# The table of tokens by expert: added up on chip by zero-one matmuls in place of scatters to DRAM

## The chip, the cores and the metric

The kernel runs on one core of a Trainium2 chip. The metric is the device time of one execution in microseconds (us). The kernel before was run three times: 811.25, 808.84 and 810.61 us, median 810.61. A further execution was profiled. PE is the matrix engine (TensorE), PEld its weight loads, DVE the vector engine, ACT the scalar engine, POOL GpSimd, SP the engine that issues most DMAs.

## What is computed

Two stages, all in float32. First a block-causal attention with 8 batches, 8 heads, 576 tokens and a head dimension of 64; its output, laid out as 4608 tokens of 512 values, goes into a mixture of experts with one expert a token.

```python
# attention: q, k, v [8, 8, 576, 64], block 64
scores = q @ k.T / 8, masked to block_i >= block_j
attn_out = softmax(scores) @ v
x = attn_out.transpose(0, 2, 1, 3).reshape(4608, 512)
# mixture of experts: E = 8, F = 1024
logits = normed(x) @ normed(expert_emb).T / tau
e = argmax(logits);  gate = softmax(logits)[e]
out[token] = gate * (relu(x[token] @ w1[e]) @ w2[e])
```

## The kernel before, in words

**Attention (0 to about 355 us).** The work is 32 passes, one for each pair of heads of a batch (n = 0 to 31, four a batch). A pass has five parts, each a Python generator: `p` prepares q and k (transposes, L326 to L345), `m` finds row maxima (L361 matmuls, L367 on DVE), `s` makes scores and their exp (five groups of matmuls L422, exp on ACT L429/L431, sums pS on POOL L400/L403), `v` multiplies with v (L457) and sums (L476), `f` finishes (L502 to L538). `l` issues the loads (L225) and stores of finished rows (L576, L578). A plan, a string of these letters written by hand for the first passes, the steady ones (n = 5 to 26) and the last (n = 27 to 31), says which generator takes its next step; `run` (L866) steps them, and the main loop (L879) goes through the passes. So the order of every engine's instructions is fixed by the plan, and parts of different passes lie beside each other. PSUM is used as four double banks (`psm`), taken from the front of a list and given back at its end (L199 to L209); a score group holds one until its exp is done.

**The route.** When the fourth pair of a batch b has finished, `route(b)` (L587) is queued in the list `slow`; the plan's letter `r` takes one of its steps, so it spreads over the passes that follow. It finds each token's expert as a zero-one row `ohb`, ranks the tokens of each expert by small matmuls (L616 to L620), adds a base of its expert (L725, `above`), squares the rows (ACT, L582), and works out in `table_rows` (L740; L745 on POOL, L747 to L752 on DVE) the place of each token in a table of tokens by expert. Tokens lie on 128 partitions, NJ = 5 to a partition for a batch. The table is `table` in DRAM with E x RE x 128 places (E = 8 experts, RE = 36 rows of 128 places for each). L670 to L680 write the batch's token numbers there: five indirect DMAs issued by POOL (L672), one for each of the five columns, one step of the route each. This is done for b = 0 to 6; the last batch is placed otherwise.

**Who reads the table.** `zeros` (L282) clears it at the start by a DMA from POOL (L284). `early_rows` (L708, after batch 5) loads the first rows of expert 0 to `et` (SP, L711), gathers those tokens' values (POOL, L717) and turns them into store indices (L694 to L697). Before the experts' part, L1243 loads the whole table as `tbt` (SP), and L1331 to L1334 transpose it on PE (`tps`) and copy it (`tsb`).

**Mixture of experts (about 358 us to the end).** 34 slots of 128 tokens; for each PE transposes the gathered tokens (L1093), multiplies with both weight matrices (L1122), ACT and DVE work on the result (L1149, L1175, L1181, L1183), POOL gathers (L1085) and stores (L1189) by indirect DMA. Nothing of it changes but the source of L1333.

Of the kernel before, what the change touches and what calls it, by code (L numbers as in the profile page):

```python
# [48 lines left out]
def kernel(  # L49
# [12 lines left out]
    nc = tc.nc  # L62
    B, H, S, D = q.shape
    E, DM, DF = w1.shape
    NT = B * S
    P = 128
    NP = H // 2
    NJ = (S - 64) // P + 1
# [5 lines left out]
    EARLY = 2  # L74
# [6 lines left out]
    dram = ctx.enter_context(tc.tile_pool(name="dram", bufs=1, space=bass.MemoryType.DRAM))  # L81
# [3 lines left out]
    RE = (NT + P - 1) // P  # L85
    NCH = (E * RE + P - 1) // P
    RC = E * RE // NCH
    assert RC * NCH == E * RE
    table = dram.tile([E * RE * P, 1], F32, name="table")


    ident = const.tile([P, P], F32, name="ident")
# [18 lines left out]
    def iota(name, shape, pattern, base=0, cm=0, dt=F32):  # L111
        t = const.tile(shape, dt, name=name)
        nc.gpsimd.iota(t, pattern=pattern, base=base, channel_multiplier=cm, allow_small_or_imprecise_dtypes=True)
        return t
# [3 lines left out]
    tokf = iota("tokf", [P, B, NJ], [[S, B], [P, NJ]], 1, 1)  # L118
    gi = iota("gi", [P, NSLOT], [[1, NSLOT]])
    pio = iota("pio", [P, P], [[1, P]])  # L120
# [12 lines left out]
    drop = const.tile([P, NJ], F32, name="drop")  # L133
# [59 lines left out]
    op = pool(left, "op", 1)  # L193
# [7 lines left out]
    def take_bank():  # L201
        return banks.pop(0) if wide else ps_b.tile([P, 2, 512], F32, name="psb")
# [4 lines left out]
    def give_bank(t):  # L207
        if wide:
            banks.append(t)  # L209
# [55 lines left out]
    nmr = [rt.tile([P, P], F32, name=f"nmr{i}") for i in range(2)]  # L265
    oe = [rt.tile([P, SP], F32, name=f"oe{i}") for i in range(2)]
    su = [rt.tile([P, 2 * P], F32, name=f"su{i}") for i in range(2)]
    zcol = op.tile([P, S], F32, name="zcol")
    nc.vector.memset(zcol, 0.0)

# [10 lines left out]

    def zeros():  # L282
        nc.gpsimd.dma_start(xbuf[0:1, :], zcol[0:1, 0:RW])
        nc.gpsimd.dma_start(table.rearrange("(c p t) o -> p c (t o)", p=RC, t=P),  # L284
                            zcol[0:RC, 0:NCH * P].rearrange("p (c t) -> p c t", t=P))
        for i in range(2):
            nc.gpsimd.memset(oe[i][:, S:SP], 0.0)
            nc.gpsimd.memset(su[i][:, LW:2 * P], 0.0)
        nc.gpsimd.memset(enT, 0.0)
        for i in range(2):  # L290
            nc.gpsimd.memset(ends_v[i][64:P], 0.0)
# [281 lines left out]
    def store_piece():  # L573
        b, xrow, j = pieces.pop(0)
        r0 = b * S + 1 + j * P
        nc.sync.dma_start(xbuf[r0:r0 + P, :], xrow[:, j, :])  # L576
        if j == NJ - 2:
            nc.sync.dma_start(xbuf[r0 + P:r0 + P + 64, :], xrow[0:64, NJ - 1, :])  # L578
# [8 lines left out]
    def route(b, xrow, lgh, ssp):  # L587
# [4 lines left out]
        ohb, acc = hot[b % 2][:, 0:NJ, :], hot[b % 2][:, NJ, :]  # L592
# [17 lines left out]
        rb = take_bank() if wide else ps_m.tile([P, 1, 512], F32, name="psm")  # L610
# [10 lines left out]
        if b < B - 1:  # L621
            t2 = above(rk, ebase)
# [28 lines left out]
        eng.tensor_scalar(ss, ss, 1.0e-6, None, op0=ALU.add)  # L651
        yield
        if b < B - 1:
            rowj = yield from table_rows(t2, ohb)
        nc.vector.reciprocal(ss, ss)
        yield
        eng.tensor_tensor(lg, lg, bc(ss.unsqueeze(2), P, NJ, E), op=ALU.mult)
# [10 lines left out]
            store(b, xrow, (NP - 1) * P, RW)  # L668
        yield
        if b < B - 1:  # L670
            for j in range(NJ):
                w = nc.gpsimd.indirect_dma_start(  # L672
                    out=table, out_offset=bass.IndirectOffsetOnAxis(ap=rowj[:, j:j + 1], axis=0),
                    in_=tokf[:, b, j:j + 1], in_offset=None, bounds_check=E * RE * P - 1, oob_is_err=False)
                for o in writes:
                    tc.declare_no_dep(w.ins, o.ins, reason="each place is written once")
                writes.append(w)
                if (b == B - 2 or j == NJ - 1) and pieces:
                    store_piece()
                yield  # L680
            if b == EB:
                early_g.append(early_rows())

    EB = B - 3
    early_g = []
    writes, ends = [], []
    ei = st.tile([P, 2, EARLY], I32, name="ei")
    ex = [st.tile([P, RW], F32, name=f"ex{u}") for u in range(EARLY)]

# [16 lines left out]
        yield  # L706

    def early_rows():  # L708
        et = rt.tile([P, EARLY], F32, name="et")
        none = rt.tile([P, EARLY], F32, name="enone")  # L710
        nc.sync.dma_start(et, table.rearrange("(p r) o -> p (r o)", p=P)[:, 0:EARLY])  # L711
        yield
        while pieces:
            store_piece()
        nc.gpsimd.tensor_copy(ei[:, 0], et)
        for u in range(EARLY):
            nc.gpsimd.indirect_dma_start(  # L717
                out=ex[u], out_offset=None, in_=xbuf[0:1 + (EB + 1) * S, :],
                in_offset=bass.IndirectOffsetOnAxis(ap=ei[:, 0, u:u + 1], axis=0))
            yield  # L720
        indices(nc.gpsimd, None, ei[:, 1], et, none)

    def above(rk, base):
        t = sm.tile([P, NJ, E], F32, name="t2")
        nc.vector.tensor_tensor(t, rk, base, op=ALU.add)  # L725
        return t
# [12 lines left out]

    def table_rows(t, ohb):  # L740

        row = sm.tile([P, NJ], F32, name="row")
        rowt = sm.tile([P, NJ], I32, name="rowt")
        rowj = sm.tile([P, NJ], I32, name="rowj")
        nc.gpsimd.tensor_tensor(t, t, ohb, op=ALU.mult)  # L745
        yield
        nc.vector.tensor_reduce(rowj, t, axis=AX.X, op=ALU.max)  # L747
        yield
        nc.vector.tensor_scalar(rowt, rowj, P - 1, None, op0=ALU.bitwise_and)
        nc.vector.scalar_tensor_tensor(row, rowj, 1.0 / P, drop, op0=ALU.mult, op1=ALU.add)  # L750
        yield
        nc.vector.scalar_tensor_tensor(rowj, rowt, float(E * RE) - 1.0 / P, row, op0=ALU.mult, op1=ALU.add)  # L752
        yield
        return rowj

    def drain(g, n=None, skip=("pe", "squares", "fine")):
        while g is not None and (n is None or n > 0):
# [82 lines left out]
    for i in range(1, NBUF):  # L840
        init_a(nc.gpsimd, qa[i])
        init_x(nc.gpsimd, qa[i], 1)
    zeros()
    drain(pb, 2)
    fill(1)
# [52 lines left out]
    def flat(ap):  # L898
        return ap.rearrange("p o n -> p (o n)")
# [300 lines left out]
    def chain():  # L1200
# [4 lines left out]
        for c in fg:  # L1205
            if c == "squares":
                break
            yield c
        ch_sq.append(fg)
        rg = route(B - 1, xrow, lgh, ssp)  # L1210
        for c in rg:
            if c == "counted":
# [26 lines left out]
        drain(g)  # L1239
    del slow[:]  # L1240
    ring(0)
    tbt = st.tile([P, NCH * RC], F32, name="tbt")
    nc.sync.dma_start(tbt, table.rearrange("(p r) o -> p (r o)", p=P))  # L1243

    mx = ctx.enter_context(tc.tile_pool(name="mx", bufs=1, reuse_waits="tile"))
    for nm in ("xh", "xl"):
# [78 lines left out]
    a, b = ea  # L1325
# [4 lines left out]
    go()  # L1330
    tps = ps_m.tile([P, 512], F32, name="psm")  # L1331
    for c in range(NCH):
        nc.tensor.transpose(tps[0:RC, c * P:(c + 1) * P], tbt[:, c * RC:(c + 1) * RC], ident)  # L1333
    nc.vector.tensor_copy(tsb, tps[0:RC, 0:NCH * P].rearrange("r (c t) -> r c t", t=P))  # L1334
    def second(c):
        split_lo(1, c, 1, to=0)
# [190 lines left out]
```

## Time and profile before

| | us |
|---|---|
| median of three runs | 810.61 |
| the profiled execution, its own time | 810.42 |
| its span in the profile | 808.7 |
| PE at work | 779.2 (96%) |
| DVE at work | 604.2 (75%) |
| POOL at work | 435.7 (54%) |
| ACT at work | 408.4 (50%) |

The granted clock of TensorE is 1.00 over the span. "Busy" leaves out register, branch and semaphore instructions. A line such as L422 is a line of the kernel. Matmul ends are modelled, so lengths of matmuls overlap; the distance of two starts is the better measure of PE's pace. In a line of the order of instructions, a group "x2" is two like instructions, and what stands in brackets is how long the engine was idle before it and what released it.

### The profile page before, as it was taken

What the parts mean: (1) busy time and instruction counts of PE and PEld (TensorE: products, weight loads), DVE (VectorE), ACT (ScalarE), POOL (GpSimd) and SP (SyncE); (2) the same over time, 40 slices, a digit from 0 to 9 for tenths busy, and PEclk for the clock granted to TensorE, in tenths of its full rate; (3) what the DMA queues carried; (4) which work ended last, traced back from release to release, by engine and by line L of the source; (5) the groups of instructions that cost most, each with busy time, mean ns of one, the idle gap of its engine ahead of it and who ended that gap; (6) DMA issues with size and microseconds to landing.
All of it is one profiled execution on the core that took longest, in us unless ns stands there. A gap on an engine that the chain in (4) does not pass through costs nothing. (4 is left out here: it accounts for less than half of the span.)

```text
span 808.7 us, 23043 instructions
## 1 busy us (share of the span) xinstructions
PE 779.2 (96%) x7160; PEld 627.3 (78%) x7160; DVE 604.2 (75%) x1382; ACT 408.4 (50%) x831; POOL 435.7 (54%) x420
## 2 busy tenths in 40 slices
PE   8999999999999998899999999999999999999997
PEld 3678878787878776668878887788888888888885
DVE  6667878686868776658868777877887778877881
ACT  2566757575757564664744456553533332543222
POOL 7555676767676757772347288784761111661110
PEclk9999999999999999999999999999999999999999
DMA  4745364545454543163845357454441111111111
GB/s 104 169 95 136 84 158 105 147 104 132 101 140 100 141 100 101 29 231 127 297 151 166 100 158 235 152 167 150 148 153 45 55 54 45 38 49 55 54 35 39
DMA packets 141421, 93.95 MB, mean 116 GB/s; under 512 B 118925, under 2 KB 120541, under 8 KB 141260
## 3 DMA queue, kind: packets, MB, share of 16 engines
q1 hardware_dynamic: 133228, 69.74, 31.2%
q0 software_dynamic: 8032, 22.36, 8.7%
q8 instruction: 66, 1.08, 0.6%
q14 instruction: 95, 0.78, 0.3%
HBM read 72.71 MB, written 19.71 MB: 114 GB/s over the span
## 5 line engine op out<-in xcount | busy, mean ns | idle before, releaser
L1175 DVE STREAM_TRANSPOSE pt<-h 32x256 f32<-32x256 f32 x528 | 240.6, 456 | 31.3 <-ACT h L1149 14.1
L367 DVE TENSOR_REDUCE nmx<-psm 128x16 f32<-128x1024 f32 (+2 forms) x128 | 125.6, 986 | 21.4 <-PE psm L361 18.5
L912 POOL TENSOR_TENSOR ring_l<-raw,ring_h 128x1024 f32 (+1 forms) x49 | 116.3, 2406 | 35.7 <-ACT ring_h L907 20.0
L1189 POOL DMA_INDIRECT out_dram<-y,outi x36 | 36.7, 1020 | 176.5 <-ACTq L1061 118.8
L1122 PE MATMUL py<-ring_h,hh 128*128 x272 | 109.3, 402 | 0.7 <-ACT h L1149 0.7
L1122 PE MATMUL py<-ring_l,hh 128*128 x272 | 106.3, 391 | 0.0
L429 ACT ACTIVATE pT<-psm 128x640 f32<-128x640 f32 (+2 forms) x128 | 89.1, 703 | 28.2 <-PE psm L361 16.8
L403 POOL TENSOR_TENSOR pS<-pS,pT 128x640 f32<-128x640 f32 (+2 forms) x93 | 93.5, 1006 | 10.9 <-ACT pT L431 3.2
L1122 PE MATMUL py<-ring_h,hl 128*128 x272 | 88.8, 389 | 0.0
L1122 PE MATMUL ph<-ring_l,xh 128*128 x280 | 86.3, 390 | 0.8 <-POOLq L1073 0.8
L1122 PE MATMUL ph<-ring_h,xh 128*128 x280 | 86.3, 389 | 0.6 <-ACTq L1061 0.6
L457 PE MATMUL psm<-pT,vo 128*64 128x320 f32 (+2 forms) x640 | 76.1, 380 | 1.0 <-issue 1.0
L1188 ACT ACTIVATE y<-py,xg 128x512 f32<-128x512 f32 x34 | 23.4, 689 | 103.5 <-PE py L1122 97.9
L1183 DVE TENSOR_TENSOR hl<-pt,hh 128x512 fp32r<-128x512 f32 x66 | 42.5, 686 | 42.0 <-ACT hh L1181 42.0
L422 PE MATMUL psm<-qh,kh 64*128 64x320 f32 (+4 forms) x384 | 66.5, 341 | 5.9 <-ACT pT L429 3.5
L907 ACT CAST ring_h<-raw 128x1024 f32 (+1 forms) x62 | 61.0, 1050 | 22.1 <-POOLq L1073 11.6
L1181 ACT CAST hh<-pt 128x512 fp32r<-128x512 f32 x66 | 35.5, 590 | 72.1 <-DVE pt L1175 71.7
L1122 PE MATMUL ph<-ring_h,xl 128*128 x280 | 69.2, 389 | 0.0
L457 PEld LDWEIGHTS psm<-pT,vo 128*64 128x64 f32 x640 | 43.2, 137 | 29.3 <-issue 1.9
L1122 PEld LDWEIGHTS ph<-ring_l,xh 128*128 128x128 f32 x280 | 52.5, 188 | 12.1 <-POOLq L1073 1.2
L1122 PEld LDWEIGHTS ph<-ring_h,xh 128*128 128x128 f32 x280 | 52.5, 188 | 11.7 <-ACTq L1061 0.8
L1122 PEld LDWEIGHTS ph<-ring_h,xl 128*128 128x128 f32 x280 | 52.6, 188 | 10.9
(289 smaller groups left out, 1680.7 us busy)
## 6 DMA issues: line engine op xcount, KB each, us to landing
raw<-in_moe_w_dram SPq DMA_DIRECT2D x60, 512.0 KB
qn<-in_q_dram SPq DMA_DIRECT2D x64, 128.0 KB
kn<-in_k_dram SPq DMA_DIRECT2D x64, 128.0 KB
vo<-in_v_dram SPq DMA_DIRECT2D x64, 128.0 KB
xbuf<-xrow SPq DMA_DIRECT2D x28, 260.0 KB
raw<-in_moe_w_dram POOLq DMA_DIRECT2D x4, 512.0 KB
qa<-nmT SPq DMA_DIRECT2D x64, 2.5 KB
xbuf<-xrow SPq DMA_DIRECT2D x7, 130.0 KB
```

The costliest lines, as they stand in the source:

```text
L367: nc.vector.tensor_reduce(m[:, :, f:f + o // w], mt[:, :, 0:o].rearrange("p h (b c) -> p h b c", c=w), axis=AX.X, op=ALU.max, negate=True)
L403: nc.gpsimd.tensor_tensor(o, o, pT[:, :, off[t]:off[t] + w], op=ALU.add)
L422: nc.tensor.matmul(st[0:kw, hh, o:o + c1 - c0], kk[hd[hh], t * P:t * P + kw], qq[hd[hh], 64 + c0:64 + c1], start=(x == 0), stop=(x == len( ...
L429: nc.scalar.activation(pT[:, :, f:f + w] if c0 else pA, st[:, :, 0:w], AF.Exp, scale=scale)
L457: m = nc.tensor.matmul(ob[hh * D:(hh + 1) * D, b0:b0 + q1 - c0], rows(vo, ends_v, n, t)[:, hh, :], pTs[hh][0][:, f0:f0 + q1 - c0] if c0 el ...
L907: return (nc.scalar.copy if eng is nc.scalar else eng.tensor_copy)(piece(ring_h, to, c, half), raw[i][:, c * CW:(c + 1) * CW])
L912: return eng.tensor_tensor(piece(ring_l, to, c, half), raw[i][:, c * CW:(c + 1) * CW], piece(ring_h, to, c, half).bitcast(F32), op=ALU.sub ...
L1122: m = nc.tensor.matmul(out, ac, slots[g]["w", i](r, c * n + off), start=(u == 0 and c == 0), stop=(c == nk - 1 and u == len(turns) - 1))
L1175: nc.vector.transpose(pt[32 * j:32 * j + 32, :, 32 * i:32 * i + 32], h[32 * i:32 * i + 32, :, j, :])
L1181: nc.scalar.copy(sets["hh"][u], pt[:, 4 * u:4 * u + 4])
L1183: nc.vector.tensor_tensor(sets["hl"][u], pt[:, 4 * u:4 * u + 4], sets["hh"][u].bitcast(F32), op=ALU.subtract)
L1189: nc.gpsimd.indirect_dma_start(out=out, out_offset=bass.IndirectOffsetOnAxis(ap=to, axis=0), in_=y, in_offset=None, bounds_check=NT - 1, o ...
```

## The change

The table is kept in SBUF as `tbt`, 128 partitions by E x RE columns, cleared by a memset on POOL. For each batch `table_rows` returns two numbers for each token: `place[:, 0]`, the partition, and `place[:, 1]`, the column. For each of the five token columns POOL makes two tables by comparison: `lane` [128 tokens x 128], which holds the token's number at its partition and zero elsewhere, and `inrow` [128 tokens x columns], which holds one at its column. Five matmuls, in the one-pass type F32R, add `lane` transposed times `inrow` up in a PSUM bank, and DVE adds the bank to `tbt`. The columns are those that a batch can have reached: rb = 5, 9, 14, 18, 23, 27, 32 rows for each of the eight experts, 40 to 256 columns. The ten POOL instructions of a batch are spread over three steps of the route; five more steps (17 for batch 6) go by before the matmuls. A route of batches 0 to 5 has 35 steps in place of 31, that of batch 6 has 47. The DMA that cleared the table, the 35 scatters and both loads of the table are gone. `et` is a view of `tbt`.

```diff
-    table = dram.tile([E * RE * P, 1], F32, name="table")
...
+    tbt = st.tile([P, E, RE], F32, name="tbt")
+    erow = op.tile([P, E, RE], F32, name="erow")
+    nc.gpsimd.iota(erow, pattern=[[RE, E], [1, RE]], base=0, channel_multiplier=0, allow_small_or_imprecise_dtypes=True)
+    lane = op.tile([P, NJ, P], F32R, name="lane")
+    inrow = op.tile([P, NJ, E * RE], F32R, name="inrow")
...
-        nc.gpsimd.dma_start(table.rearrange("(c p t) o -> p c (t o)", p=RC, t=P),
-                            zcol[0:RC, 0:NCH * P].rearrange("p (c t) -> p c t", t=P))
+        nc.gpsimd.memset(tbt, 0.0)
...
         if b < B - 1:
+            rb = -(-(b + 1) * S // P)
+            here = inrow[:, :, 0:E * rb]
             for j in range(NJ):
-                w = nc.gpsimd.indirect_dma_start(
-                    out=table, out_offset=bass.IndirectOffsetOnAxis(ap=rowj[:, j:j + 1], axis=0),
-                    in_=tokf[:, b, j:j + 1], in_offset=None, bounds_check=E * RE * P - 1, oob_is_err=False)
...
+                nc.gpsimd.tensor_scalar(here[:, j].rearrange("p (e r) -> p e r", e=E), erow[:, :, 0:rb],
+                                        place[:, 1, j:j + 1], None, op0=ALU.is_equal)
+                nc.gpsimd.tensor_scalar(lane[:, j], pio, place[:, 0, j:j + 1], tokf[:, b, j:j + 1],
+                                        op0=ALU.is_equal, op1=ALU.mult)
                 if (b == B - 2 or j == NJ - 1) and pieces:
                     store_piece()
+                if j % 2 or j == NJ - 1:
+                    yield
+            for _ in range(17 if b == B - 2 else 5):
                 yield
+            bank = take_bank()
+            new = bank[:, 0, 0:E * rb]
+            for j in range(NJ):
+                nc.tensor.matmul(new, lane[:, j], here[:, j], start=(j == 0), stop=(j == NJ - 1))
+            nc.vector.tensor_tensor(tbt[:, :, 0:rb], tbt[:, :, 0:rb], new.rearrange("p (e r) -> p e r", e=E), op=ALU.add)
+            give_bank(bank)
+            yield
...
-        et = rt.tile([P, EARLY], F32, name="et")
+        et = tbt[:, 0, 0:EARLY]
-        nc.sync.dma_start(et, table.rearrange("(p r) o -> p (r o)", p=P)[:, 0:EARLY])
...
+        place = sm.tile([P, 2, NJ], F32, name="place")
...
-        nc.vector.scalar_tensor_tensor(rowj, rowt, float(E * RE) - 1.0 / P, row, op0=ALU.mult, op1=ALU.add)
+        nc.vector.tensor_copy(place[:, 0], rowt)
+        nc.vector.scalar_tensor_tensor(place[:, 1], rowt, -1.0 / P, place[:, 1], op0=ALU.mult, op1=ALU.add)
...
-    tbt = st.tile([P, NCH * RC], F32, name="tbt")
-    nc.sync.dma_start(tbt, table.rearrange("(p r) o -> p (r o)", p=P))
```

## Rows read from the trace of the kernel before

**Rows 1.** Page, busy us (share of the span) x instructions of each engine.

```profile
PE 779.2 (96%) x7160; PEld 627.3 (78%) x7160; DVE 604.2 (75%) x1382; ACT 408.4 (50%) x831; POOL 435.7 (54%) x420
```

**Rows 2.** Stretches: length; busy PE, PEld, DVE, ACT, POOL; clock, DMA share, GB/s.

```profile
66.65:76.19 9.54, 9.54 (x159) 8.09 (x157) 7.21 (x17) 5.91 (x13) 6.37 (x7) 1.00 0.65 148
...
96.32:107.39 11.07, 10.27 (x158) 8.13 (x156) 7.61 (x19) 6.08 (x15) 8.41 (x9) 1.00 0.46 124
107.39:116.90 9.51, 9.51 (x158) 8.05 (x156) 7.19 (x17) 5.73 (x12) 7.37 (x8) 1.00 0.72 144
178.79:190.07 11.28, 10.03 (x158) 7.97 (x156) 7.54 (x19) 6.05 (x14) 8.39 (x10) 1.00 0.45 120
190.07:200.38 10.31, 9.87 (x159) 7.97 (x156) 7.20 (x17) 5.76 (x13) 7.76 (x8) 1.00 0.59 143
```

**Rows 3.** Order in time, pass n = 16: start, length, engine, line, [idle before <- releaser].

```profile
182.25 1.08 POOL L672 DMA_INDIRECT table<-tokf,rowj  x1 [0.27 <-issue]
...
182.82 0.28 PE L422 MATMUL psm<-qa,ka 64*128 64x256 f32 x2
...
183.60 0.60 ACT L429 ACTIVATE pA<-psm 128x512 f32<-128x512 f32 x1 [1.01 <-PE psm L422]
183.63 0.97 POOL L672 DMA_INDIRECT table<-tokf,rowj  x1 [0.30 <-issue]
...
185.11 0.70 ACT L429 ACTIVATE pT<-psm 128x640 f32<-128x640 f32 x1 [0.92 <-PE psm L361]
```

**Rows 4.** Order in time, pass n = 18.

```profile
204.41 0.28 PE L422 MATMUL psm<-qa,ka 64*128 64x256 f32 x2
...
204.76 0.60 ACT L429 ACTIVATE pA<-psm 128x512 f32<-128x512 f32 x1 [0.53 <-PE psm L422]
```

**Rows 5.** Order in time around the second early gather.

```profile
325.23 0.96 POOL L717 DMA_INDIRECT ex<-xbuf,ei  x1 [0.30 <-issue]
...
326.97 1.52 ACT L429 ACTIVATE pT<-psm 128x640 f32<-128x640 f32 x2 [0.99 <-PE psm L361]
```

**Rows 6.** Order in time beside the scatters of batches 5 and 6.

```profile
308.52 0.55 PE L457 MATMUL psm<-pT,vo 128*64 128x192 f32 x4 [0.96 <-issue]
...
311.12 0.47 PE L361 MATMUL psm<-kh,qh 64*128 64x448 f32 x2 [1.03 <-issue]
...
349.24 0.32 ACT L502 COPY su<-psm 128x192 f32<-128x192 f32 x1 [2.32 <-PE psm L422]
```

**Rows 7.** Order in time in the experts' part.

```profile
447.21 1.01 POOL L1189 DMA_INDIRECT out_dram<-y,outi  x1 [2.02 <-ACT hh L1181]
...
447.39 1.09 ACT L1149 ACTIVATE h<-ph 128x512 f32<-128x512 f32 x2 [0.61 <-PE ph L1122]
```

**Rows 8.** Groups by line and shape: count | busy us, mean ns | idle before, releaser.

```profile
L403 POOL TENSOR_TENSOR pS<-pS,pT 128x640 f32<-128x640 f32 x31 | 48.2, 1553 | 3.9 <-ACT pT L429 1.9
...
L672 POOL DMA_INDIRECT table<-tokf,rowj x35 | 35.2, 1005 | 9.9 <-issue 9.5 <-ACT oe L463 0.2
...
L345 DVE TENSOR_TENSOR ql<-psm,qh 128x640 fp32r<-128x640 f32 x32 | 26.1, 816 | 14.5 <-ACT qh L343 14.5
...
L403 POOL TENSOR_TENSOR pS<-pS,pT 128x128 f32<-128x128 f32 x31 | 14.2, 459 | 2.4
...
L907 POOL CAST ring_h<-raw 128x1024 fp32r<-128x1024 f32 x6 | 6.7, 1117 | 3.4 <-DMA raw<-in_moe_w_dram 2.7 <-PE psm L1093 0.7
...
L651 POOL TENSOR_SCALAR ss<-ss 128x5 f32<-128x5 f32 x7 | 1.7, 245 | 0.6
```

**Rows 9.** Order in time, PE at the front of the experts' part.

```profile
363.51 0.39 PE L1122 MATMUL psm<-ring_l,xh 128*128 128x512 f32 x1
363.74 0.39 PE L1122 MATMUL psm<-ring_h,xh 128*128 128x512 f32 x1
```

**Rows 10.** Instructions of L725: ns least/median/most, first and last start, shape.

```profile
L725 DVE TENSOR_TENSOR t<-psm,ebase x7: 199/200/201, 84.1 to 338.5; 128x40 f32<-128x40 f32 x7
```

**Rows 11.** Waits by waiting line and releaser: total us, count, mean us.

```profile
SPq L1243 <- DMA table<-tokf,rowj: 3.6, 1, 3.6
```

More of the change, by code (lines that the diff above doesn't have):

```diff
@@ L653, in route @@
         if b < B - 1:
-            rowj = yield from table_rows(t2, ohb)
+            place = yield from table_rows(t2, ohb)
         nc.vector.reciprocal(ss, ss)
@@ L670, in route @@
         if b < B - 1:
+            rb = -(-(b + 1) * S // P)
+            here = inrow[:, :, 0:E * rb]
             for j in range(NJ):
-                w = nc.gpsimd.indirect_dma_start(
-                    out=table, out_offset=bass.IndirectOffsetOnAxis(ap=rowj[:, j:j + 1], axis=0),
-                    in_=tokf[:, b, j:j + 1], in_offset=None, bounds_check=E * RE * P - 1, oob_is_err=False)
-                for o in writes:
-                    tc.declare_no_dep(w.ins, o.ins, reason="each place is written once")
-                writes.append(w)
+                nc.gpsimd.tensor_scalar(here[:, j].rearrange("p (e r) -> p e r", e=E), erow[:, :, 0:rb],
+                                        place[:, 1, j:j + 1], None, op0=ALU.is_equal)
+                nc.gpsimd.tensor_scalar(lane[:, j], pio, place[:, 0, j:j + 1], tokf[:, b, j:j + 1],
+                                        op0=ALU.is_equal, op1=ALU.mult)
                 if (b == B - 2 or j == NJ - 1) and pieces:
                     store_piece()
+                if j % 2 or j == NJ - 1:
+                    yield
+            for _ in range(17 if b == B - 2 else 5):
                 yield
+            bank = take_bank()
[5 more added lines that the diff above has]
+            yield
             if b == EB:
@@ L685 @@
     early_g = []
-    writes, ends = [], []
+    ends = []
     ei = st.tile([P, 2, EARLY], I32, name="ei")
@@ L740, in table_rows @@
     def table_rows(t, ohb):
-        row = sm.tile([P, NJ], F32, name="row")
+        rowj = sm.tile([P, NJ], I32, name="rowj")
         rowt = sm.tile([P, NJ], I32, name="rowt")
-        rowj = sm.tile([P, NJ], I32, name="rowj")
+        place = sm.tile([P, 2, NJ], F32, name="place")
         nc.gpsimd.tensor_tensor(t, t, ohb, op=ALU.mult)
@@ L749, in table_rows @@
         nc.vector.tensor_scalar(rowt, rowj, P - 1, None, op0=ALU.bitwise_and)
-        nc.vector.scalar_tensor_tensor(row, rowj, 1.0 / P, drop, op0=ALU.mult, op1=ALU.add)
+        nc.vector.scalar_tensor_tensor(place[:, 1], rowj, 1.0 / P, drop, op0=ALU.mult, op1=ALU.add)
         yield
-        nc.vector.scalar_tensor_tensor(rowj, rowt, float(E * RE) - 1.0 / P, row, op0=ALU.mult, op1=ALU.add)
+        nc.vector.tensor_copy(place[:, 0], rowt)
+        nc.vector.scalar_tensor_tensor(place[:, 1], rowt, -1.0 / P, place[:, 1], op0=ALU.mult, op1=ALU.add)
         yield
-        return rowj
+        return place
     def drain(g, n=None, skip=("pe", "squares", "fine")):
@@ L1332 @@
     for c in range(NCH):
-        nc.tensor.transpose(tps[0:RC, c * P:(c + 1) * P], tbt[:, c * RC:(c + 1) * RC], ident)
+        nc.tensor.transpose(tps[0:RC, c * P:(c + 1) * P], flat(tbt)[:, c * RC:(c + 1) * RC], ident)
     nc.vector.tensor_copy(tsb, tps[0:RC, 0:NCH * P].rearrange("r (c t) -> r c t", t=P))
```

## The prediction

> **What bounds the kernel now.** The busy line of the page comes first: PE is at work for 96% of the span, POOL for 54% [rows 1]. The kernel is bound by PE, so an edit counts only by the PE work it adds or by PE idle time that it takes away or makes. The second view is busy time by stretch, and I cut the attention part into its passes, one for each head pair n (a pass starts at the same instruction of the plan each time). A pass without a route takes 9.54 us and PE is never idle in it (n = 5); the pass that holds the first three scatters of a batch takes 11.07 us for batch 0 (n = 8) and 11.28 us for batch 2 (n = 16), with PE idle for 0.80 and 1.25 us [rows 2]. Batches 1, 3 and 4 (n = 12, 20, 24) read 11.28 us too. The pass behind, which holds scatters 4 and 5, takes 9.51 us for batch 0 and 10.31 us for batch 2 [rows 2].
>
> The third view, the order of instructions in time, says what the idle time is made of. In n = 16 PE issues the last matmul of the first score group at 182.82 us; ACT, which has nothing else to do, starts its exp at 183.60 us, 0.78 us later, after 1.01 us of waiting. All that time POOL issues a scatter (182.25 us, for 1.08 us). The next exp waits 0.92 us while the second scatter is issued [rows 3]. In n = 18, with no scatter, the same pair of instructions stands 0.35 us apart [rows 4]. PE then waits for the bank that the late exp holds. I went through every wait of another engine for a PE completion between 60 and 352 us: all those in which more than 0.62 us pass between the matmul's start and the waiter's lie at most 2 us behind the start of an indirect DMA, a scatter of L672 or a gather of L717. The two gathers are the cleaner case, for no load of q, k or v goes beside them: the exp at 326.97 us, behind the gather at 325.23 us, had waited 0.99 us [rows 5].
>
> So the forecast rests on this reading: while POOL issues an indirect DMA in the attention part, others learn of PE's completions about half a microsecond late, and in this tight rotation of four banks that comes back to PE. The change takes 35 of the 37 such DMAs there away.
>
> **The change part by part: what it takes away.** (a) Scatters 1 to 3 of batches 0 to 4. Their pass should fall to that of a plain pass with a little route work, 9.65 us: 11.07 − 9.65 = 1.4 us once and 11.28 − 9.65 = 1.6 us four times, 7.8 us [rows 2]. It is 5 us if only the three waits' excess comes back (about 1 us a pass), 8.6 if the pass falls to 9.51. (b) Scatters 4 and 5: 10.31 − 9.54 = 0.8 us in four passes at most, but batch 0 has the same two scatters and 9.51 us, so part of it is another thing; I take 0.5 each, 2.0 us (0 to 3.1). (c) Batch 5, in another plan of the passes: two idle times of PE, 0.96 and 1.03 us, stand beside its scatters, 2.0 us (1 to 2.4) [rows 6]. (d) Batch 6: ACT waits 2.32 us for PE behind two scatters [rows 6], but here the table's new work stands close to its use, and PE's matmuls may come to wait for POOL's tables; I take 0.8 of it (between 2.3 gained and 1 lost). Sum: 7.8 + 2.0 + 2.0 + 0.8 = 12.6 us gained.
>
> **What it adds on PE.** Seven times five matmuls, of 40, 72, 112, 144, 184, 216 and 256 columns (8 experts by the table rows that the batch can have reached): 1024 columns each for the five lanes, 5120 in all. Columns go at 0.23 us per 512, read as the distance of two starts [rows 9], 0.45 ns each: 2.3 us. Each also has 128 columns of weights to load, 0.06 us by the same rate, 35 × 0.06 = 2.1 us where nothing hides it. I take half of it, 3.3 us. Batch 6's share, some 0.7 us, stands where PE waits for ACT's squares, so 2.6 us. Bounds: 2.0 us, and 35 × 0.28 = 9.8 us by the recorded length of a matmul of 256 columns, which overlaps its neighbours [rows 3]; I stay near the first, because a start-to-start distance is what a queue of PE pays.
>
> **What it moves on POOL.** Gone: 35 scatters, 35.2 us of work and 9.5 us of issue idle, 44.7 us [rows 8]. New: 35 tables of 128 columns and 35 of 40 to 256. No row has this operation; the nearest are a one-input operation on 5 columns, 0.245 us, and a cast of 1024, 1.117 us [rows 8], which make 0.24 us + 0.85 ns a column: 35 × 0.35 + 35 × 0.24 + 5120 × 0.85 ns = 25 us. With the two-input sum's 459 ns at 128 columns and 1553 ns at 640 (0.19 us + 2.14 ns) [rows 8] it is 34 us. Either is less than what goes. In the order of POOL the ten of a batch replace the three scatters that stand ahead of the pass's sums pS: 3.1 to 5.6 us in place of 3 × 1.28 = 3.8 us. The matmuls come eight steps of the route later, about a pass [rows 2], so they wait for no table; the cover is about 10 us of other work.
>
> **What it adds on DVE.** One add out of PSUM a batch, 40 to 256 columns: 0.20 us at 40 [rows 10], 0.82 us at 640 [rows 8], so 0.2 to 0.42 us, 2.2 us in all, and a copy of five columns a batch. DVE waits for ACT or PE in every pass; I cost it at nothing. Without that cover it is up to 3 us. The matmuls take a bank and give it back behind that add; two or three of the four stand free there, so the next score group finds one.
>
> **The other transfers.** The zeroing of the table, the early load and the late load of the table: SP waits 3.6 us for the last scatter at the late one [rows 11], but the transposes that use it come right behind other PE work. Nothing.
>
> One rule of the Trainium skill speaks against (a) to (d). Its page "SBUF — State Buffer", section "Who interferes with whom", says that a DMA never contends with a compute engine and that PE and ACT never wait on anyone there. By it the scatters' issue would delay nobody; what else then delays is rival 1. The 0.78 against 0.35 us of rows 3 and 4 doesn't prove it wrong, since two things go beside each other in n = 16.
>
> **The sum.** −12.6 + 2.6 = −10.0 us: 810.42 us, the profiled execution's time (span 808.7 and 1.7 around it), becomes 800.4. The median of the three runs is 810.61, 0.19 above; from it, 800.6 us. All ends against me: −5 −0 −1 +1 +4 = −1 us, 809.6. All for me: −8.6 −3.1 −2.4 −2.3 +2.0 = −14.4 us, 796.2.
>
> **Rivals.** 1, slower: the late completions come not from the scatters but from the transfers that land then. Loads of q, k and v and stores of xrow stand on SP's queue beside the scatters of n = 16. For it: in the MoE part, ACT starts its pass over ph 0.18 us after an indirect store's issue began with only 0.61 us waited, no longer than elsewhere [rows 7]. Against it: the gathers have no such loads beside them and the wait is there. Then nothing is gained and the PE work is lost, 2.6 to 4 us: 813.2 to 814.6. It is so if the pass n = 16 keeps its 11.2 us without its scatters. 2, half: the exps start in time, but the pass then ends on another wait of its chain (the route's ACT step waiting for POOL, DVE's longer queue), and half of (a) to (c) comes back: 6.3 − 1.5 = about 5 us, 805.5. 3, slower: POOL's compare costs far more than a cast. From 0.9 us each the ten fill the pass, and above it the sums pS and the matmuls are late; at 1.2 us each it is 3 us a batch, 21 us less the 10 gained, 822. The two prices a column worked out above speak against it, 0.24 to 0.74 us for a table.
>
> **How the numbers follow.** The forecast gets 0.66, rival 1 0.13, rival 2 0.13, rival 3 0.05; 0.03 is left for a gain larger than the sum. About 0.3%, 2.4 us, can be told from no change, so "same" is 808.2 to 813.0. Faster: 0.64 of the forecast, rival 2 and the rest, 0.80. Same: 0.02 of the forecast's end, 0.04 of rival 1, 0.01 of rival 3, 0.07. Slower: 0.13. The range goes from the sum's best end, 796.0, over rival 2 to 808.5, just under the forecast's worst; it leaves out rivals 1 and 3.
>
> **What would show it.** Right: passes of 9.6 to 9.9 us at n = 8, 12, ... 24, the exp of n = 16 starting 0.35 us behind its matmul, late completions left beside the two gathers alone, POOL's tables at 0.25 to 0.5 us, five matmuls in 0.3 to 0.9 us with no wait ahead. Wrong: passes still at 11 us with no scatter in them (rival 1), PE waiting for lane or inrow (rival 3), PE idle elsewhere in the same pass (rival 2).

## The result, and the profile after

The changed kernel takes 819.46 us (median of six runs, 816.96 to 821.15), the kernel before in the same comparison 809.76 us (six runs, 808.27 to 811.78). The ratio is 1.0116 with a 95% interval of 1.0091 to 1.0140: 9.7 us slower, where 10 us faster was forecast. The profiled execution of the changed kernel took 817.99 us and its span is 816.3 us, 7.6 us above the span before.

The busy line of the page, of the changed kernel:

```profile
PE 785.3 (96%) x7195; PEld 635.4 (78%) x7195; DVE 604.9 (74%) x1396; ACT 409.4 (50%) x831; POOL 451.5 (55%) x456
```

POOL has 15.8 us more to do; by the forecast it would have had 1 to 10 us less [rows 1]. Where the 7.6 us came from is read by setting the starts of like instructions of both traces side by side; a minus says that the changed kernel is ahead.

| instruction | before, us | after, us | difference |
|---|---|---|---|
| first exp of pass n = 8 | 100.69 | 100.62 | −0.07 |
| first exp of n = 27 | 298.65 | 291.09 | −7.56 |
| first exp of n = 28 | 310.42 | 301.42 | −9.00 |
| first exp of n = 29 | 324.46 | 318.95 | −5.51 |
| first exp of n = 31 | 346.31 | 340.76 | −5.55 |
| first transpose of the early rows (L1093) | 352.05 | 350.70 | −1.35 |
| first matmul of the experts' part | 358.29 | 358.85 | +0.56 |
| first cast of a gathered slot | 406.29 | 407.51 | +1.22 |
| last output store | 804.39 | 806.35 | +1.96 |
| end of the span | 808.7 | 816.3 | +7.6 |

So the forecast gain comes: 9.0 us up to n = 28. Then 3.5 us go in one pass, 4.2 us between n = 31 and the early rows, 2.6 us on the way to the first gathered slot, 0.7 us in the slots, and 5.6 us behind the last store, where nothing is computed any more. The four rows below are the changed kernel's busy times by stretch (columns as in rows 2; a pass is cut here at its first exp): n = 8 and n = 16, which hold a batch's tables and matmuls, n = 17, and n = 28.

```profile
100.62:110.94 10.32, 10.32 (x165) 8.57 (x163) 7.52 (x18) 5.88 (x12) 9.79 (x14) 1.00 0.51 136
180.73:191.09 10.36, 10.36 (x165) 8.58 (x163) 7.54 (x18) 5.89 (x13) 10.20 (x13) 1.00 0.51 135
191.09:200.61 9.52, 9.52 (x160) 8.07 (x158) 7.55 (x20) 5.93 (x13) 6.03 (x8) 1.00 0.66 146
301.42:318.95 17.53, 14.85 (x211) 11.64 (x209) 11.20 (x24) 6.58 (x15) 12.77 (x16) 0.90 0.29 85
```

In the steady passes PE is busy from end to end: the idle time of 0.80 to 1.25 us of [rows 2] is gone, and the pass behind takes 9.52 us where it took 10.31. What is left of the pass above 9.5 us is PE's own work for the five matmuls, 0.8 to 0.9 us. In n = 28 PE is idle for 2.7 us and its granted clock is 0.90. The next view, the order in time, has the cause; the last two of the five matmuls of batch 5 wait for POOL:

```profile
297.45 0.83 POOL L677 TENSOR_SCALAR inrow<-erow,place 128x216 fp32r<-128x216 f32 x1
298.27 0.80 POOL L679 TENSOR_SCALAR lane<-pio,place,tokf 128x128 fp32r<-128x128 f32 x1
...
302.17 0.57 PE L690 MATMUL psm<-inrow,lane 128*128 128x216 f32 x3
303.88 0.37 PE L690 MATMUL psm<-inrow,lane 128*128 128x216 f32 x1 [1.14 <-POOL lane L679]
304.61 0.79 POOL L679 TENSOR_SCALAR lane<-pio,place,tokf 128x128 fp32r<-128x128 f32 x1
...
305.46 0.36 PE L690 MATMUL psm<-inrow,lane 128*128 128x216 f32 x1 [1.22 <-POOL lane L679]
```

POOL makes the ten tables from 297.45 to 305.40 us, PE comes to them at 302.17 us. Batch 6 goes the same way, 338.77 to 347.23 us against 343.39 us, with two waits of 1.30 us:

```profile
343.39 0.90 PE L690 MATMUL psm<-inrow,lane 128*128 128x256 f32 x3
345.60 0.39 PE L690 MATMUL psm<-inrow,lane 128*128 128x256 f32 x1 [1.30 <-POOL lane L679]
347.28 0.38 PE L690 MATMUL psm<-inrow,lane 128*128 128x256 f32 x1 [1.30 <-POOL lane L679]
```

Behind both, the stretches show TensorE granted 0.50 (1.2 GHz in place of 2.4), after the stretches with the waits:

```profile
304.00:307.00 3.00, 1.78 (x28) 1.40 (x30) 1.07 (x2) 0.32 (x1) 2.93 (x3) 0.99 0.09 35
307.00:310.00 3.00, 3.00 (x32) 2.64 (x28) 2.01 (x5) 1.30 (x2) 1.46 (x2) 0.50 0.00 0
346.00:348.00 2.00, 0.72 (x5) 0.60 (x7) 0.14 (x1) 0.00 (x0) 1.75 (x5) 0.97 0.00 0
348.00:350.00 2.00, 1.96 (x24) 1.83 (x20) 1.29 (x5) 0.70 (x1) 0.42 (x3) 0.50 0.06 14
350.00:352.00 2.00, 1.30 (x6) 1.30 (x7) 0.39 (x1) 2.00 (x4) 2.00 (x3) 0.50 1.02 367
352.00:354.00 2.00, 2.00 (x14) 1.29 (x14) 2.00 (x2) 0.53 (x1) 2.00 (x3) 0.50 0.54 111
```

The groups by line and shape (columns as in rows 8) give the price of a table: 0.80 us for a lane, 0.39 to 0.92 us for an inrow, 50.6 us in all (the lanes' 27.9 and the seven inrow groups together 22.7, of which the first and the last stand here).

```profile
L679 POOL TENSOR_SCALAR lane<-pio,place,tokf 128x128 fp32r<-128x128 f32 x35 | 27.9, 798 | 0.0
...
L677 POOL TENSOR_SCALAR inrow<-erow,place 128x256 fp32r<-128x256 f32 x5 | 4.6, 924 | 0.0
...
L677 POOL TENSOR_SCALAR inrow<-erow,place 128x40 fp32r<-128x40 f32 x5 | 2.0, 392 | 0.0
```

The end, last: POOL's sequencer runs three DRAIN instructions behind the last store, and the longest took 2.54 us before and takes 6.85 us after (ns least/median/most, first and last start). It does not wait for the last store to land: that store's last recorded packet had moved by 808.62 us, and from 808.7 to 815.4 us the DMA share is 0.00 and no engine is busy. The kernel before first, then the changed one.

```profile
L1522 POOLq DRAIN  x3: 46/109/2544, 805.3 to 808.4; - x3
```

```profile
L1533 POOLq DRAIN  x3: 46/103/6853, 808.6 to 816.0; - x3
```

### The profile page after: what moved, and what is told of

Its sections match the earlier page's. It is cut to its first block, busy times and chain, and to the rows that moved or that the text cites. A ratio compares the mean times of both kernels' runs of the same rounds, so it can differ in the third digit from the quotient of the medians.

```text
span 816.3 us, 23111 instructions
## 1 busy us (share of the span) xinstructions
PE 785.3 (96%) x7195; PEld 635.4 (78%) x7195; DVE 604.9 (74%) x1396; ACT 409.4 (50%) x831; POOL 451.5 (55%) x456
## 5 line engine op out<-in xcount | busy, mean ns | idle before, releaser
L370 DVE TENSOR_REDUCE nmx<-psm 128x16 f32<-128x1024 f32 (+2 forms) x128 | 125.7, 986 | 11.8 <-PE psm L364 8.9
L432 ACT ACTIVATE pT<-psm 128x640 f32<-128x640 f32 (+2 forms) x128 | 89.3, 703 | 24.1 <-PE psm L364 11.8
L406 POOL TENSOR_TENSOR pS<-pS,pT 128x640 f32<-128x640 f32 (+2 forms) x93 | 93.5, 1005 | 10.4 <-ACT pT L432 4.3
```

Source lines behind the costliest of these rows:

```text
L370: nc.vector.tensor_reduce(m[:, :, f:f + o // w], mt[:, :, 0:o].rearrange("p h (b c) -> p h b c", c=w), axis=AX.X, op=ALU.max, negate=True)
L406: nc.gpsimd.tensor_tensor(o, o, pT[:, :, off[t]:off[t] + w], op=ALU.add)
L432: nc.scalar.activation(pT[:, :, f:f + w] if c0 else pA, st[:, :, 0:w], AF.Exp, scale=scale)
```

## The experiments

The runs went to several chips, and they differ for the kernel before: on two of them it took 794 us (794.2, median of seven runs), on the others 809 to 811 us, as in its first profile. So each experiment is compared with the kernel before on its own chip, and the changed kernel with itself.

**The changed kernel again**, unchanged.

> The changed kernel as it is, a second look at its profile. In the first look POOL's last drain, after the last store, lasted 6.85 us (2.54 us in the kernel before) and the time from the last store's issue to the end of the span was 9.95 us (4.3 us before). If this end belongs to the change, it is 9 to 14 us here again; if it is chance, it can fall to 4.3 us and the span to about 811. The pass of n = 28 should again be 17.5 us long and the way from the first exp of n = 31 to the first matmul of the experts' part 20.5 us.

It took 817.44 us on a chip where the kernel before takes 794.21: there it is 23 us slower. The end is the same to 10 ns (the drain 6.85 us, 9.9 us behind the last store), n = 28 takes 17.60 us. The way from n = 31 to the experts' part takes 18.1 us in both traces; the 20.5 us of the expectation was no reading of the first trace (358.85 − 340.76 = 18.1). It is not chance, and the two chips' changed kernels are alike; it is the kernel before that differs.

**The kernel before without scatters.**

```diff
             for j in range(NJ):
-                w = nc.gpsimd.indirect_dma_start(out=table, ..., in_=tokf[:, b, j:j + 1], ...)
-                ...
                 if (b == B - 2 or j == NJ - 1) and pieces:
```

> The kernel before without its 35 scatters and with nothing in their place, so the table stays zero and the experts' part gathers one row everywhere: its time is read in the attention part alone. Theory (scatters' issue on POOL delays what others learn of PE): passes n = 8 and n = 12 to 24 fall from 11.1 to 9.5 to 9.7 us, the passes behind from 10.3 to 9.5, and n = 28 starts 11 to 12 us earlier than before. Rival (landing loads and stores cause it): passes stay at 11 us. The end: if few DMAs of POOL make its last drain long, it is over 6 us here too; if it is the tables that POOL makes, it is 2.5 us.

Measured on the same chip: 797.21 us, 3 us more than the kernel before there; its end alone, 10.38 us behind the last store, is 6.2 us longer than the 4.18 us of the kernel before in the next run. Pass n = 8:

```profile
100.00:109.51 9.51, 9.51 (x160) 8.03 (x158) 7.26 (x17) 5.89 (x12) 5.26 (x5) 1.00 0.49 135
```

The passes fall to 9.51 us and n = 28 starts 14.0 us earlier than in the first profile of before, as the theory has it. But a kernel without 35 scatters that is not faster than the kernel with them on that chip can't be explained by it, and the last drain was 7.03 us without any table on POOL. Both asked for the kernel before itself on such a chip.

**The kernel before, profiled there.**

> The kernel before, unchanged, profiled beside the experiments. On the chip of the first four of them it took 794.2 us, 16 us less than in its first profile, though the changed kernel took the same as before. Theory: the late PE completions beside POOL's indirect DMAs are there on one chip and not on another; where it takes 794 us, the passes n = 8 and n = 12 to 24 take 9.5 us with their scatters in them, and the exps behind the two early gathers wait under 0.5 us. Rival: the time is saved elsewhere (in the experts' part or at the end), and the passes with scatters still take 10.9 to 11.1 us. The last drain of POOL is 2.54 us either way.

794.84 us. Its trace, first n = 8 and n = 16 by stretch, then the rows of the scatter and the exp that answer to [rows 3]:

```profile
100.36:109.88 9.52, 9.52 (x160) 8.05 (x158) 7.26 (x17) 5.89 (x13) 8.33 (x9) 1.00 0.50 134
178.72:188.23 9.51, 9.51 (x160) 8.03 (x158) 7.25 (x17) 5.89 (x12) 8.24 (x9) 1.00 0.51 133
```

```profile
177.77 1.08 POOL L672 DMA_INDIRECT table<-tokf,rowj  x1 [0.27 <-issue]
...
178.37 0.28 PE L422 MATMUL psm<-qa,ka 64*128 64x256 f32 x2
...
178.72 0.60 ACT L429 ACTIVATE pA<-psm 128x512 f32<-128x512 f32 x1 [0.58 <-PE psm L422]
```

The scatter is issued in the same place and for the same 1.08 us, and the exp starts 0.35 us behind its matmul, not 0.78. The passes with scatters take 9.5 us with scatters in them. The late completions are real on one chip and absent on another, for the same program. (That the chip itself makes the difference, and not something that went with it, is not shown.) The changed kernel shows the same at its second early gather, first in the trace of the result, then in the trace of "the changed kernel again":

```profile
320.00 0.96 POOL L729 DMA_INDIRECT ex<-xbuf,ei  x1 [0.30 <-issue]
...
321.40 1.51 ACT L432 ACTIVATE pT<-psm 128x640 f32<-128x640 f32 x2 [0.81 <-PE psm L364]
```

```profile
319.41 0.96 POOL L729 DMA_INDIRECT ex<-xbuf,ei  x1 [0.30 <-issue]
319.42 2.82 ACT L432 ACTIVATE pT<-psm 128x640 f32<-128x640 f32 x4
```

On this chip the change has nothing to gain; what it costs is all that is left, 23 us. The run without scatters therefore decides nothing between its theory and its rival, for here the passes take 9.5 us either way.

**Lanes of batches 5 and 6 on DVE.**

```diff
-                nc.gpsimd.tensor_scalar(lane[:, j], pio, ...
+                (nc.vector if b >= EB else nc.gpsimd).tensor_scalar(lane[:, j], pio, ...
```

> Of batches 5 and 6 alone, the five tables of 128 columns are made on DVE, the rest as in the changed kernel. Theory: PE waits at the matmuls of these two batches because ten tables take POOL 8.1 and 8.6 us there and the plan leaves 4 to 5 us. Then POOL's part falls to 4.1 and 4.6 us, both waits go, TensorE's clock stays at 1.00 from 300 to 360 us, n = 28 takes 14 instead of 17.5 us, the way from n = 31 to the experts' part 14 instead of 20.5 us: 9 to 10 us less than the changed kernel, about 810. Rival (what makes these stretches long is the DVE add or the bank, not POOL's tables): no more than 2 us less.

814.38 us, 3 us less than the changed kernel on that chip instead of 9 to 10. (The 817.44 us are one run, and the four runs here range from 812.26 to 817.59.) n = 28 takes 13.96 us as expected, with no wait for a table; the theory holds for that pass. For batch 6 the waits for tables are gone too, but the way from n = 31 to the experts' part takes 16.8 us and not 14: PE then waits 1.81 us for an exp of ACT, and the granted clock falls to 0.50 there (348 to 352 us) all the same. And the pass n = 27 grew from 10.33 to 15.72 us; DVE's rows say how that begins. The ten instructions by line (ns least/median/most) took 0.28 to 1.57 us:

```profile
L679 DVE TENSOR_SCALAR lane<-pio,place,tokf x10: 284/412/1569, 294.9 to 341.9; 128x128 fp32r<-128x128 f32 x10
```

In the order in time, DVE's and POOL's rows there:

```profile
294.88 2.00 DVE L679 TENSOR_SCALAR lane<-pio,place,tokf 128x128 fp32r<-128x128 f32 x2
...
295.26 1.53 POOL L404 TENSOR_TENSOR pS<-pT 128x640 f32<-128x640 f32 x1
...
296.80 0.15 DVE L535 TENSOR_SCALAR rin<-psm 128x8 f32<-128x8 f32 x1
```

The second lane takes 1.57 us and is done at 296.88 us, when POOL's sum ends (295.26 + 1.53 = 296.79), and what is queued behind it on DVE is late. How the 1.3 us lost there become 5.4 us of the pass is not shown. That two such engines hold each other up is what the Trainium skill says (page "SBUF — State Buffer", section "Who interferes with whom": DVE's two-port modes and GpSimd share a port pair, and the later one stands still until the other is done); these rows agree with it. But the other nine lanes, most of them beside POOL's own tables, took only 0.28 to 0.53 us, so not every overlap costs that much, and no row shows in which mode DVE ran.

**Idle matmuls in the waits.**

```diff
                 nc.tensor.matmul(new, lane[:, j], here[:, j], start=(j == 0), stop=(j == NJ - 1))
+                if b >= EB and 1 < j < NJ - 1:
+                    for _ in range(6):
+                        nc.tensor.matmul(bank[:, 1, 0:512], onesb, bc(onesb.unsqueeze(1), P, 4, P), ...)
```

> The changed kernel with six idle matmuls of 512 columns behind the third and the fourth of the five matmuls of batches 5 and 6; they fill PE's waits and their result is not used. It tells the wait from what the clock costs behind it. Theory: about 6 of the 10 us lost behind n = 28 are waits, some 4 us are TensorE at 0.50 for 3 and for 7 us behind them. Then the clock stays at 1.00, the waits stay, and the way is 3 to 5 us shorter: about 815. If the waits alone cost the time, nothing changes.

813.63 us against 817.44 of the changed kernel on that chip, 3.8 us less, though PE does 24 matmuls more. The stretch behind batch 5's waits keeps its clock:

```profile
307.00:310.00 3.00, 2.83 (x51) 2.41 (x50) 2.52 (x7) 1.89 (x4) 1.83 (x4) 1.00 0.02 5
```

Both are single runs, but the stretches bear them out: the pass n = 28 gives 0.8 us of it, the way from n = 31 to the first matmul of the experts' part 2.8 us. So of what is lost from n = 28 on about 4 us is the clock, the rest of the loss up to the experts' part the waits.

**Matmuls of batches 5 and 6 later.**

```diff
-            for _ in range(17 if b == B - 2 else 5):
+            for _ in range(24 if b == B - 2 else 9 if b == EB else 5):
```

> The changed kernel with the matmuls of batch 5 four steps later and those of batch 6 seven steps later; POOL's work is the same. Theory: PE waits for POOL's tables there, and four steps, 4 to 5 us, are enough for batch 5, so n = 28 takes 14 us instead of 17.5; for batch 6 only 1.2 us of matmuls come to lie ahead, so of its 4.2 us some 1 to 1.5 go. About 4 us less than the changed kernel. If something else makes n = 28 long, it stays at 17.5 us.

806.48 us, 11 us less than the changed kernel (817.44, on another chip of the 794 us kind), not 4. n = 28 takes 13.67 us, 0.9 us more than the 12.79 us of the kernel before on that chip:

```profile
301.48:315.15 13.67, 12.94 (x211) 10.21 (x207) 11.22 (x24) 6.57 (x14) 12.67 (x16) 1.00 0.38 107
```

That is the theory's 3.9 us. From n = 31 to the early rows it takes 7.6 us (10.0 in the changed kernel's trace from a chip of this kind), PE waits 0.91 and 1.29 us there, and the clock stays at 1.00 from 300 to 350 us, which I had not counted on: the way from there to the first matmul of the experts' part is 1.8 us shorter too. Why it stays with these waits and not with two of 1.30 us is not shown. 3.6 us more are saved in the slots, most of it at waits for gathered rows; that is partly luck, for the changed kernel's own two traces differ by 1.4 us there.

**35 scatters put back.** They go into the five steps behind the tables and write to a table that nobody reads.

> The changed kernel with 35 scatters of the kernel before put back into the steps behind the tables; they write to a table in DRAM that nobody reads. All kernels with 78 indirect DMAs of POOL had a last drain of 6.85 to 7.03 us and 9.9 to 10.4 us from the last store to the end, the kernel before with 113 had 2.54 and 4.3 us. If the number of these DMAs sets the length of the end, it is back to 4.3 us here; if it is the missing zeroing, the place of the last store or anything else that the two kernels don't share, it stays at 9.9 us. Passes with scatters: 10.3 us and more where PE's completions are late beside them, 9.5 and 10.3 us (with matmuls) where they aren't.

833.34 us, against an expectation of passes of 9.5 and 10.3 us: passes of up to 15.5 us stand among the steady ones (n = 10 takes 15.3), so POOL's tables, sums and scatters together seem to be too much for one pass. The drain, though, is short again:

```profile
L1542 POOLq DRAIN  x3: 46/109/2372, 828.3 to 831.4; - x3
```

The end is 4.2 us behind the last store, as before. So it is not the tables, the missing zeroing or the place of the last store that make the end long; the missing scatters do, by their number or by something that goes with them.

**How it hangs on their number**, with spare DMAs in the experts' part, on the kernel with the later matmuls:

```diff
             in_=y, in_offset=None, bounds_check=NT - 1, oob_is_err=False)
+        if g < 35:      # 17 in the second kernel
+            nc.gpsimd.indirect_dma_start(out=spare, ..., in_=y[:, 0:1], ...)
```

> As the one with the spare DMAs, with 17 of them, 95 indirect DMAs of POOL in all. It asks how the last drain hangs on their number: 6.85 us at 78, 2.4 to 2.5 us at 113. If it falls in proportion it is about 4.7 us; if there is a number from which it is short, it is 6.85 or 2.4 us.

> The kernel with the later matmuls and, behind each of the 34 output stores of the experts' part, one more indirect DMA of POOL that writes one column of y to a spare place in DRAM; POOL has idle time there. Theory: with 112 of these DMAs in place of 78 the end behind the last store falls from 9.9 to 4.2 us and nothing else changes: 5.7 us less, some 801. On a chip where the kernel before takes 794 us that is 0.8% slower, on one where it takes 810 us it is 1.1% faster. If the last drain doesn't hang on the number but on DMAs in the attention part, it stays at 6.85 us; if the spare DMAs hold POOL up, the slots take longer than 11.35 us.

With 17 (95 in all, 851.34 us) the drain is longer still:

```profile
L1538 POOLq DRAIN  x3: 46/108/8327, 840.5 to 849.4; - x3
```

8.33 us for 95 and 6.85 us for 78 are 0.088 us a DMA each; both my alternatives were wrong. With 113 in the kernel before it is 2.5 us, as if something started anew between 95 and 113. With 35 spare ones (113) the drain was 6.92 us, so the number alone does not settle it. That run was disturbed: it took 862.12 us against 809.46, because POOL's output stores waited for earlier landings and the gathers came late, with 39 us of idle PE between 400 and 840 us, 30 of them waits for gathered rows. The instruction of POOL's queue just ahead of the drain (INC_SWDGE_SEM) was short as in the kernels with 113 (0.48 us, 1.84 with 78); why the drain was not, stays open. Their attention part says what the chip of the 809 us kind gives to the later matmuls: n = 31 starts at 336.75 us, 9.6 us ahead of the first profile of before.

**The fifth column's tables of batch 6 on DVE**, on top of that kernel.

> As the one with the spare DMAs, but of batch 6 the two tables of the fifth column are made on DVE. POOL is done with its eight 1.7 us earlier, so of the waits of 0.90 and 1.29 us ahead of the fourth and fifth matmul most goes: 1.5 to 2 us less. Rival: DVE's table operations stand still while POOL works, as in the run where DVE made all lanes of batches 5 and 6 (0.28 to 1.57 us for 128 columns), and the gain is under 1 us.

859.57 us, 2.6 us less than with POOL alone. One of the two waits in batch 6 is gone (1.03 us is left of 0.92 and 1.29), the first matmul of the experts' part comes at 349.2 us in place of 352.2. The two operations on DVE took 0.32 and 0.41 us and hold nothing up in that place; among the ten, one did. (The runs of the two kernels overlap, 859.86 to 864.57 and 855.19 to 860.62 us; the stretches carry the reading.)

**The same without spare DMAs, and with spare DMAs that wait for nothing.**

```diff
+        if spare and g < NSLOT:
+            nc.gpsimd.indirect_dma_start(out=spare.pop(), ..., in_=tokf[:, 0, 0:1], ...)   # second kernel only
```

> The kernel with the later matmuls (batch 5 four steps, batch 6 seven) in which DVE makes the two tables of batch 6's fifth column; no spare DMAs. From the stretches of the runs so far: attention to the first matmul of the experts' part at 349.2 us on a chip with late completions, then as in the kernel with the later matmuls 455.2 us to the end, 9.9 us of end among them: 804.5 us of span, 806.2 us. Against 809.5 us of the kernel before that is 0.4% faster on such a chip; on a chip where the kernel before takes 794 us it is about 804, 1.3% slower.

> The same with 34 spare DMAs in the experts' part that wait for nothing and that nothing waits for: 128 token numbers to a place of their own in DRAM, behind each output store. In the runs with spare DMAs of y the next output store waited for earlier landings (6.79 us at 521 us) and the slots grew. Theory: without that wait the slots keep 11.35 us and the end falls from 9.9 to 4.2 us, 5.7 us less, 800.5 us. Rival: it is POOL's DMAs themselves that delay the gathers, and the slots are long again (over 840 us).

Both ran on one chip of the 809 us kind. The kernel without spare DMAs takes 806.75 us against 810.61, ratio 0.9952 (0.9933 to 0.9971): half a per cent or 3.9 us faster, as expected (806.2). On a chip of the 794 us kind the kernel with the later matmuls takes 806.5 us, 1.6% more than the kernel before. The one with spare DMAs takes 841.6 us: the drain is 2.93 us with 112 indirect DMAs, so the end is nearly repaired (5.1 us behind the last output store, 4.2 expected), and the DMAs that repair it need not stand in the attention part. But the slots are long again. The spare DMAs wait for nothing, yet five output stores still waited 35 us in all for landings of earlier ones (7 us without spare DMAs), and the gathers came late. One of them, from its issue to the matmul that waits for its rows:

```profile
505.87 0.99 POOL L1102 DMA_INDIRECT xg<-xbuf,rowi  x1 [0.31 <-POOLq L1090]
...
514.61 1.11 PE L1110 MATMUL px<-ident,xg 128*128 128x128 f32 x4 [6.17 <-DMA xg<-xbuf,rowi]
```

The gathers' packets of 4160 bytes took 1.2 us each on average in the slots, against 0.23 us without spare DMAs. What the spare DMAs do to the DMA engines shows best in a stretch in which PE is busy throughout in both kernels, 680 to 720 us, the kernel with spare DMAs first, then the one without:

```profile
680.00:720.00 40.00, 40.00 (x183) 33.08 (x182) 33.03 (x69) 14.17 (x28) 11.10 (x10) 1.00 0.53 47
```

```profile
680.00:720.00 40.00, 40.00 (x184) 33.09 (x183) 32.64 (x69) 19.33 (x33) 24.90 (x14) 1.00 0.13 40
```

The share of the DMA engines goes from 0.13 to 0.53 for a few KB more: with 128 writes of four bytes ahead of each gather, the gathers are slow. My rival was right here (841.6, over 840), and no cheap way to give the end its 5.7 us back was found.

## Why the prediction failed, point by point

**The reading that carried the forecast** (completions are late while POOL issues an indirect DMA) was right for the chip that it was read on. From n = 8 to n = 27 the kernel before needs 197.96 us there and 186.19 us on a chip without the lateness, 11.8 us; terms (a) and (b) said 9.8. The changed kernel needs 190.47, which is 7.5 less, and 5 × 0.85 us of PE work for its matmuls account for the rest. That the five passes then take 10.3 to 10.4 us, and not the forecast's 9.6 to 9.9, is this work. For (c), n = 27 and 28 together take 25.81 us against 23.11 us, 2.7 us (2.0 forecast); for (d), n = 31 to the early rows 5.74 against 4.49, 1.25 us (0.8). Together 15.8 us, not 12.6: all four terms were somewhat small, none was wrong. Rival 1, the landing loads, is out for that chip: they land in the changed kernel too, and no pass has a late completion but at the two early gathers, which it keeps (the exp there waited 0.81 us, [rows 5] 0.99). The landing of the scatter is out as well for the exp of [rows 3]: that scatter's first recorded packet moves at about 184.3 us, behind the late start at 183.60. Rival 2 is out, for PE is idle nowhere in the five passes; its price was a slip besides, since half of the gain less the sum's own 2.6 us of PE work is 3.7 and not 5 us. That the lateness comes and goes with the chip, no row of one trace could have said; why stays open. On the others the rule of the Trainium skill that I weighed against the rows (page "SBUF — State Buffer", section "Who interferes with whom") is what one sees: the 0.35 us beside a scatter there agree with it, the 0.78 us of [rows 3] don't.

**PE's matmuls: the term was mis-sized.** 3.3 us were forecast for 35, with half of their weight loads hidden. A pass grows by 0.80 to 0.88 us whether they have 40 or 184 columns, 6.0 us for seven batches. From the first of the five of batch 2 to the next other matmul it is 0.69 us, for those of 40 columns 0.67 us, and the middle ones start 0.11 us apart at 40 to 216 columns alike. So it is not the columns that are paid but something that each matmul has, most likely its new weights, which the forecast had at 0.06 us and half hidden; no run separates the weights from other fixed costs:

```profile
188.68 0.77 PE L690 MATMUL psm<-inrow,lane 128*128 128x112 f32 x5
...
189.37 0.55 PE L460 MATMUL psm<-pT,vo 128*64 128x192 f32 x4
```

**POOL's tables: the step that failed.** "The matmuls come eight steps of the route later, about a pass [rows 2], so they wait for no table; the cover is about 10 us of other work." This was read from the steady passes and holds there: 9.1 us from the first table to the first matmul, against 5.8 to 7.6 us for the ten tables. For batches 5 and 6 I had put the same distance, although the last plans take a step of the route much more often (27 to 31 steps a pass, the steady plan 11): from the first table to the first matmul it is 4.7 and 4.6 us (in batch 6 with 20 steps between them), and the ten tables take 8.0 and 8.5 us. All tables cost 50.6 us, not 25 to 34: 0.80 us for 128 columns with two operations, and (0.924 − 0.392) / 216 = 2.5 ns a column with one. My lower price came from a cast, 0.85 ns a column; of the two neighbours, the two-input sum with 2.14 ns a column [rows 8] was the near one. Even at 34 us in all, a table pair of batch 6 would have been 0.46 + 0.74 = 1.2 us, ten tables 6.0 us against 4.6: the wait could be had from the rows, if the distance had been looked up for each batch. Rival 3 is this mechanism, but I had put its threshold at 0.9 us a table for all batches; here it was a matter of two batches.

**What the wait costs** was missing but for batch 6's bound. Batch 5 costs 3.9 us above its matmuls (17.53 against 13.67, where they come later), batch 6 4.6 us (9.94 − 4.49 − 0.85). Both hold some of the clock's loss: with idle matmuls in the waits they are 0.8 and 1.0 us less. On the way to the first gathered slot 2.6 us more go, of which 1.9 us are the clock (8.15 us from the early rows to the first matmul of the experts' part, 6.25 with idle matmuls); the other 0.7 us were not there in the changed kernel's second trace. The forecast had a bound of 1 us for all of batch 6 and none for batch 5.

**The end** was not in the sum: "Nothing", for the DMAs that fall away outside the passes. It costs 5.6 us, and the trace of before held only a drain of 2.54 us, from which nobody could read that with fewer DMAs it would be longer.

The terms as measured: −15.8 gained; +6.0 matmuls, +3.9 and +4.6 waits with the clock's loss in them, +2.6 on the way to the first gathered slot, +0.8 a later gather at the ninth slot, +5.6 the end, 23.5 together. −15.8 + 23.5 = +7.7 us, against 7.6 us between the two spans (each term is a difference of the same traces, so that the sum comes out is no proof of the causes; those rest on the runs above); and +23.5 without the gain, against 23.2 us (817.44 − 794.21) on a chip without the lateness.

**DVE's adds and the early transfers** went as forecast: 0.20 to 0.42 us an add, and no wait of the table's transposes.

## What to carry to other kernels

Work that is moved onto another engine has to be set against the distance to its user for each of its places, not for the usual one; a plan that is denser at its end has shorter distances there, and a wait on the bounding engine can cost its clock as well, as those in batches 5 and 6 did here (granted 0.50 behind them). A stall that one trace shows beside a DMA can belong to the chip; before a rewrite for its sake, the same program is worth running on a second chip.

## What the runs showed of the hardware

- The same program took 794 us on two chips and 809 to 811 us on others. Between the traces of a chip of each kind it arises where POOL issues an indirect DMA beside a tight chain of PE and ACT: 17.5 us up to the first matmul of the experts' part, of which 2 us come back in the slots. There a waiter of PE started 0.78 us behind its matmul on one chip and 0.35 us on the other.
- POOL's last drain took 6.85 us (7.03 in one kernel) with 78 indirect DMAs of POOL, 8.33 us with 95 (one run), 0.088 us a DMA in both, and 2.4 to 2.9 us with 112 or 113 in three kernels; but 6.92 and 6.37 us in two kernels with 113 whose output stores and gathers were disturbed. What sets it stays open; in the changed kernel's 6.85 us no packet moves.
- A GpSimd comparison against one number a partition costs 0.39 us at 40 columns and 0.92 us at 256; with a second operation 0.80 us at 128.
- 128 four-byte writes by an indirect DMA, one in each slot of 11.35 us, raised the share of the DMA engines from 0.13 to 0.53 (680 to 720 us) and went with late gathers, 31 us of idle PE between 400 and 800 us.
